# Attention: the PV matmuls of a half unit in two bursts instead of four single chunks

## The chip, the cores and the metric

One core of one Trainium2 chip runs the whole program. The metric is the device time of one execution in microseconds (us), the median of several runs; lower is better. Where a profile is shown, it is one profiled execution. The engines are TensorE (PE; its weight loads are shown apart as PEld), VectorE (DVE), ScalarE (ACT), GpSimd (POOL) and SyncE (SP), whose queue issues the DMAs.

## What is computed

Attention over 4 batches and 8 heads (sequence 576, head size 64) with a bias that depends on positions, then two MLPs one after the other on the attention's output (2304 tokens, width 512). All data are float32.

```python
scores = scale * np.matmul(q, k.transpose(0, 1, 3, 2))
...
scores = scores + bias.transpose(2, 0, 1)[None, :, :, :]
scores = scores - np.max(scores, axis=-1, keepdims=True)
attn = np.exp(scores)
attn = attn / (np.sum(attn, axis=-1, keepdims=True) + 1e-09)
return np.matmul(attn, v).astype(np.float32)
...
x = np.ascontiguousarray(attn_out.transpose(0, 2, 1, 3)).reshape(B * S, H * D)
x = _moe_ref(x=x, **moe_kwargs)
return _moe2_ref(x=x, **moe2_kwargs)
```

## The kernel before

The program has three stages: the bias tables (until about 85 us), the attention (until about 370 us) and the two MLPs. All three are written as one order of instructions by hand: each engine works through its own queue in the order in which the Python code issues, and semaphores between engines are set from the tiles that they share.

The attention works on 16 units. A unit is a pair of heads (0 to 3) and a batch (0 to 3), with 9 query tiles: tiles 0 to 7 are 128 queries of one of the two heads in turn, tile 8 is the last 64 queries of both heads together and has twice the score matmuls. The loop over `tau` takes one step for each tile of each unit (144 steps), and 16 steps more that drain the pipeline. `u, t = divmod(tau, 9)`. In step `tau` the code issues for tiles of different age:

- `expo` (L253, ACT), for the tile of two steps ago: the exponential, with its row sums; ahead of it nothing, behind it whatever copy out of PV was put off (`late`);
- `stats` and `norm` (L257, L258 on DVE; L263 on POOL), five steps old: the reciprocals, and the scaling of the tile;
- `settle5` (L308, ACT), eight steps old: copies the fifth transposes out of PSUM;
- `reduce_min` (L246, DVE), one step old: adds the bias to the scores, negates, takes the row minimum;
- `scores` (L231, PE), the tile of this step, into one of two PSUM buffers (`ps_s`); so a step's scores need the reduction of two steps ago;
- `settle` (L303; L301 for tile 8), eight steps old: copies four transposed blocks out of PSUM into `at`, on ACT for tiles 1, 3, 5, 7 and on DVE for the others;
- the PV steps, if any are in the list `pvq`;
- `transposes` (L273, four blocks; L277 a fifth one, called F in the prediction, after each odd tile; L281 and L282 for tile 8), seven steps old, into one of two PSUM buffers.

Then follow casts of the next units' queries and keys (`high` on ACT or DVE, `low` on POOL), their loads, and parts of the MLP weights' preparation (L490 ACT; L505, L506, L507, L503 DVE; L523 ACT; L521 POOL).

PV is done per half unit: half 0 are the queries of tiles 0 to 3 (N = 256), half 1 those of tiles 4 to 8 (N = 320). When the last tile of a half is settled (tile 3 or 8), `pv_steps` appends six entries to `pvq`: chunks 0 to 4 and `evac`. Chunk 0 (L320) is one matmul with a full 128x128 weight. Each of the chunks 1 to 4 (L323) is two matmuls, one for each head, with a 128x64 weight each (shown as 128\*64): the first head's output goes to the first 64 partitions of the accumulator, the second's to the other 64. In float32 one matmul is recorded as two, so a chunk has four records. The accumulator is one PSUM buffer (`ps_v`, one buffer). `evac` (L327, ACT) copies it out and stores it to `xs` in DRAM; it isn't issued where it is popped, but in the next step behind `expo`.

What the change touches is how many entries of `pvq` are taken in a step: one, or two where more than four are in the list, and none behind an `evac`. With six entries for each half, and a half finished every five or four steps, chunks 0 and 1 come in one step, chunks 2, 3 and 4 in one step each, `evac` in the next; eight of a unit's nine steps have a PV chunk.

In the steps from 140 on `tail` starts the MLPs between the last steps of the attention (`AT`): loads of their input `xm` from `xs` (L561), their split (L567 ACT, L568 POOL), and the first blocks of matmuls `up` (L582), which share PE, ACT, DVE and POOL with what the attention still has.

Of the kernel before, what the change touches and what calls it, by code (L numbers as in the profile page):

```python
# [126 lines left out]
def attention_phase(tc, qT, kT, vP, ident_d, par, c_log, bsc, xs, after_bias, load_weight, filler, tail):  # L127
# [4 lines left out]
    with ExitStack() as st, ExitStack() as early:  # L132
        right = lambda n, k: st.enter_context(tc.tile_pool(name=n, bufs=k, side="right"))
        vp, np_, sm, xp = right("p1v", 4), right("p1n", NBUF), right("p1m", 3), right("p1x", 2)
        left = lambda n, k: early.enter_context(tc.tile_pool(name=n, bufs=k))
# [98 lines left out]
        def reduce_min(u, t):  # L234
            s = sc.pop((u, t))
            if t == 8:
                n = np_.tile([128, S], F32, name="n8", bufs=1)
            else:
                if t % 2 == 0:
                    npair[u, t // 2] = np_.tile([128, 2 * S], F32, name="n")  # L240
                n = npair[u, t // 2][:, S * (t % 2):S * (t % 2) + S]
            if t % 3 == 0:
                nmin[u, t // 3] = sm.tile([128, 3], F32, name="mn")
                nsum[u, t // 3] = sm.tile([128, 3], F32, name="sums")
            m = nmin[u, t // 3][:, t % 3:t % 3 + 1]
            V.tensor_tensor_reduce(n.rearrange("p (a b) -> p a b", a=2), s[:, :, 0:288],  # L246
                                   bias[t].rearrange("p (a b) -> p a b", a=2), -0.125, 3.0e38, ALU.add, ALU.min, m)
            ntile[u, t] = n

        def expo(u, t):  # L250
            n = ntile[u, t]
            m = nmin[u, t // 3][:, t % 3:t % 3 + 1]
            A.activation(n, n, AF.Exp, bias=m, scale=-1.0, accum_out=nsum[u, t // 3][:, t % 3:t % 3 + 1])  # L253

        def stats(u, g):
            r = sm.tile([128, 3], F32, name="rec")
            V.tensor_scalar(r, nsum[u, g], 1e-9, None, ALU.add)  # L257
            V.reciprocal(r, r)  # L258
            nrec[u, g] = r

        def norm(u, t):
            n = ntile[u, t]
            G.tensor_scalar(n, n, nrec[u, t // 3][:, t % 3:t % 3 + 1], 1.0, ALU.mult, ALU.mult)  # L263
# [32 lines left out]
        def settle(u, t):  # L296
            o, i = place(at[u, min(t // 4, 1)][0], t, tr.pop((u, t)))
            copy = A.copy if t in ON_ACT else V.tensor_copy
            if t == 8:
                for c in range(0, 4, 2):  # L300
                    copy(o[:, c:c + 2], i[:, c:c + 2])  # L301
            else:
                copy(o, i)  # L303

        def settle5(u, t):
            if t in (1, 3, 5, 8):
                o = place5(at[u, min(t // 4, 1)][1], t)
                (A.copy if t in ON_ACT5 else V.tensor_copy)(o, tf.pop((u, t))[:, 0:o.shape[1]])  # L308

        def pv_steps(u, g):  # L310
            hp, b = units[u]
            v = vs.pop(u) if g else vs[u]
            main, rest = at[u, g]
            N = GW[g]
            p = []

            def mm(c):
                if c == 0:
                    p.append(ps_v.tile([128, 512], F32, name="pv"))
                    T.matmul(p[0][:, 0:N], v[:, 4].rearrange("p a d -> p (a d)"), rest, start=True, stop=False)  # L320
                    return
                for a in range(2):
                    T.matmul(p[0][64 * a:64 * a + 64, 0:N], v[:, c - 1, a], main[:, c - 1, a * N:a * N + N], start=False, stop=(c == 4))  # L323

            def evac():
                x = xp.tile([128, 320], F32, name="x")
                A.copy(x[:, 0:N], p[0][:, 0:N])  # L327
                c0 = b * S + 256 * g
                nc.sync.dma_start(xs[128 * hp:128 * hp + 128, c0:c0 + N], x[:, 0:N])
            return [lambda c=c: mm(c) for c in range(5)] + [evac]  # L330

        pvq, late = [], []
        for tau in range(NU * 9 + TAIL):
            u, t = divmod(tau, 9)
            for _ in range(PER[min(tau, len(PER) - 1)]):
                next(bias_steps, None)
            if tau == LAG - 1:
                assert next(bias_steps, 1) == 1
                p0.close()
                at_pool = right("p1a", 1)  # L340
                ps_t, ps_f, ps_v = psr(st, "ps_t", 2), psr(st, "ps_f", 1), psr(st, "ps_v", 1)

            def at_lag(lag):
                z = tau - lag
                return divmod(z, 9) if 0 <= z < NU * 9 else None
            y = at_lag(2)
            if y:
                expo(*y)
            for f in late:
                f()  # L350
            late = []
            y = at_lag(LAG - 2)
            if y:
                if y[1] % 3 == 0:
                    stats(y[0], y[1] // 3)
                norm(*y)
            z = at_lag(LAG + 1)
            if z:
                settle5(*z)
            y = at_lag(1)  # L360
            if y:
                reduce_min(*y)
                hp, b = units[y[0]]
                if b == NB - 1 and hp + 1 < NP:
                    load_bias(hp + 1, y[1])
            if tau < NU * 9:
                scores(u, t)
            if z:
                settle(*z)
            for _ in range(2 if len(pvq) > 4 else 1):  # L370
                if pvq:
                    f = pvq.pop(0)
                    if f.__name__ == "evac":
                        late.append(f)
                        break
                    f()
            if z and z[1] in (3, 8):
                pvq += pv_steps(z[0], z[1] // 8)
            y = at_lag(LAG)
            if y:  # L380
                transposes(*y)
            if t == 0 and u + 1 < NU:
                alloc(u + 1)
            if t == 6 and u + 1 < NU:
                load_v(u + 1)
            for n, i in ((u + 1, HIGH.get(t)), (u, HIGH.get(t + 9))):
                if i is not None and 1 <= n < NU:
                    high(n, i)
            for n, i in ((u + 1, LOW.get(t)), (u, LOW.get(t + 9))):
                if i is not None and 1 <= n < NU:  # L390
                    low(n, i)
                    if n + 1 < NU:
                        load_raw(n + 1, i)
            if tau < NU * 9:
                filler(t)
            if tau == NU * 9:
                early.close()
            tail(tau - NU * 9)


TAIL = 16
NBUF = 5
EBUF = 4
LR = (16, 19, 22, 25)
# [477 lines left out]
```

## Time and profile before

| | us |
|---|---|
| median of 3 runs | 1243.32 (1241.55 to 1244.18) |
| the profiled execution, its own time | 1237.99 |
| its span, first to last instruction | 1236.2 |

| engine | busy us | share of the span |
|---|---|---|
| PE (matmuls) | 1208.7 | 98% |
| PEld (weight loads) | 1044.5 | 84% |
| DVE | 726.0 | 59% |
| ACT | 646.0 | 52% |
| POOL | 566.2 | 46% |

The table counts an engine as busy from an instruction's start to its end; matmuls are pipelined, so that PE shows as busy also where two of them overlap only a little. The shares are over all three stages. For one stage one reads the table of stretches (busy time of each engine between two times), the waits in that stretch, and the timeline, where the distance from the start of one group of matmuls to the start of the next tells what the group costs PE, whatever the lengths of its records.

### The profile page before, as it was taken

What the parts mean: (1) busy time and instruction counts of PE and PEld (TensorE: products, weight loads), DVE (VectorE), ACT (ScalarE), POOL (GpSimd) and SP (SyncE); (2) the same over time, 40 slices, a digit from 0 to 9 for tenths busy, and PEclk for the clock granted to TensorE, in tenths of its full rate; (3) what the DMA queues carried; (4) which work ended last, traced back from release to release, by engine and by line L of the source; (5) the groups of instructions that cost most, each with busy time, mean ns of one, the idle gap of its engine ahead of it and who ended that gap; (6) DMA issues with size and microseconds to landing.
All of it is one profiled execution on the core that took longest, in us unless ns stands there. A gap on an engine that the chain in (4) does not pass through costs nothing.

```text
span 1236.2 us, 21193 instructions
## 1 busy us (share of the span) xinstructions
PE 1208.7 (98%) x7856; PEld 1044.5 (84%) x7856; DVE 726.0 (59%) x1292; ACT 646.0 (52%) x1338; POOL 566.2 (46%) x584
## 2 busy tenths in 40 slices
PE   7899999999989999999999999999999999999998
PEld 2257666666659999999999999889999999999997
DVE  7898878888738988988988668961101111111010
ACT  6897777778737667677666555332112211221111
POOL 1059888888635555565555335452122221222211
PEclk9999999999999999999999999999999999999999
DMA  5765746474211333333343223421001010010000
GB/s 192 245 199 159 217 138 202 140 214 148 88 53 60 113 120 106 104 120 120 128 145 116 98 69 108 153 73 35 27 10 35 2 35 26 10 35 10 26 18 17
DMA packets 80631, 120.86 MB, mean 98 GB/s; under 512 B 10256, under 2 KB 55056, under 8 KB 80528
## 3 DMA queue, kind: packets, MB, share of 16 engines
q1 hardware_dynamic: 80528, 119.51, 30.7%
q8 instruction: 62, 1.02, 0.3%
q14 instruction: 41, 0.34, 0.1%
HBM read 89.71 MB, written 29.77 MB: 97 GB/s over the span
## 4 chain that ended last, share of the span: by engine, by line
PE 66%; DVE 3%; DMA 1%; ACT 1%; issue 1%; POOL 0%; SPq 0%; DVEq 0%; ACTq 0%; POOLq 0%
PE up L582 38%; PE acc L659 16%; PE acc L667 11%; DMA wraw<-in_wo 1%; DVE wu L507 1%; DVE wu L503 1%; DVE wu L506 0%; PE pv L323 0%; DVE wu L505 0%; DMA wraw<-in_wv 0%; ACT wu L490 0%; ACT z L601 0%; DMA xm<-xs 0%; POOL xt L568 0%; DVE o L685 0%
## 5 line engine op out<-in xcount | busy, mean ns | idle before, releaser
L582 PE MATMUL up<-xt,w 128*128 128x256 f32 (+1 forms) x3744 | 536.2, 299 | 3.9 <-DVE t L627 1.9
L582 PEld LDWEIGHTS up<-xt,w 128*128 128x128 f32 x3744 | 524.7, 190 | 15.9 <-DVE t L629 4.5
L637 POOL TENSOR_TENSOR gl<-t,gh 128x256 fp32r<-128x256 f32 (+1 forms) x204 | 184.4, 914 | 468.9 <-ACT gh L636 301.4
L629 DVE TENSOR_TENSOR t<-up,t 128x256 f32<-128x256 f32 x108 | 45.5, 422 | 318.9 <-ACT t L608 318.9
L608 ACT ACTIVATE t<-up 128x256 f32<-128x256 f32 x108 | 41.5, 384 | 327.9 <-PE up L582 327.9
L659 PE MATMUL acc<-gh,w 128*128 128x384 f32 x768 | 195.7, 335 | 2.9 <-ACT z L601 2.9
L659 PEld LDWEIGHTS acc<-gh,w 128*128 128x128 f32 x768 | 138.0, 188 | 4.7 <-ACT z L601 3.8
L667 PE MATMUL acc<-w,gh 128*128 128x512 f32 x432 | 135.6, 395 | 0.0
L263 POOL TENSOR_SCALAR n<-n,rec 128x576 f32<-128x576 f32 x144 | 114.8, 809 | 43.3 <-DVE rec L258 30.0
L659 PE MATMUL acc<-gl,w 128*128 128x384 f32 x384 | 128.4, 334 | 0.0
L253 ACT ACTIVATE n<-n,mn 128x576 f32<-128x576 f32 x144 | 112.1, 779 | 26.1 <-DVE mn L246 26.0
L246 DVE CUSTOM_DVE_ANT_0 n<-sc,bias 128x576 f32<-128x576 f32 x144 | 107.5, 747 | 15.4 <-PE sc L231 11.5
L273 PEld LDWEIGHTS pt<-ident,n 128*128 128x128 f32 x576 | 60.6, 140 | 54.9 <-issue 39.7
L568 POOL TENSOR_TENSOR xt<-xm,xt 128x384 fp32r<-128x384 f32 (+1 forms) x84 | 75.5, 911 | 68.0 <-ACT xt L567 68.0
L521 POOL TENSOR_TENSOR w<-wu,w 128x512 fp32r<-128x512 f32 x68 | 98.2, 1445 | 12.4 <-ACT w L523 11.0
L636 ACT CAST gh<-t 128x256 fp32r<-128x256 f32 (+1 forms) x204 | 91.4, 454 | 7.6 <-PE acc L659 3.6
L273 PE MATMUL pt<-ident,n 128*128 128x128 f32 x576 | 94.1, 286 | 0.9 <-DVE at L303 0.9
L323 PE MATMUL pv<-at,vs 128*64 128x320 f32 (+1 forms) x512 | 90.9, 436 | 0.0
L622 ACT ACTIVATE z<-z,c 128x768 f32<-128x768 f32 x48 | 45.2, 941 | 77.4 <-DVE up L621 77.4
L623 DVE TENSOR_TENSOR t<-up,t 128x768 f32<-128x768 f32 x48 | 45.9, 956 | 65.3 <-ACT t L601 65.3
L667 PE MATMUL acc<-w,gl 128*128 128x512 f32 x216 | 84.0, 389 | 0.0
L667 PEld LDWEIGHTS acc<-w,gh 128*128 128x128 f32 x432 | 74.5, 190 | 9.8
(70 smaller groups left out, 1683.9 us busy)
## 6 DMA issues: line engine op xcount, KB each, us to landing
wraw<-in_wo SPq DMA_DIRECT2D x28, 512.0 KB, 3.8
bsc<-e SPq DMA_DIRECT2D x36, 295.5 KB, 2.8
raw<-in_qT SPq DMA_DIRECT2D x64, 144.0 KB, 3.5
raw<-in_kT SPq DMA_DIRECT2D x64, 144.0 KB, 3.1
xm<-xs SPq DMA_DIRECT2D x48, 192.0 KB, 3.7
x2s<-o SPq DMA_DIRECT2D x48, 192.0 KB, 3.8
wraw<-in_wi SPq DMA_DIRECT2D x16, 512.0 KB, 4.3
wraw<-in_wg SPq DMA_DIRECT2D x12, 512.0 KB, 3.7
```

The source lines that it names most:

```text
L246: V.tensor_tensor_reduce(n.rearrange("p (a b) -> p a b", a=2), s[:, :, 0:288], bias[t].rearrange("p (a b) -> p a b", a=2), -0.125, 3.0e38, ...
L253: A.activation(n, n, AF.Exp, bias=m, scale=-1.0, accum_out=nsum[u, t // 3][:, t % 3:t % 3 + 1])
L263: G.tensor_scalar(n, n, nrec[u, t // 3][:, t % 3:t % 3 + 1], 1.0, ALU.mult, ALU.mult)
L273: T.transpose(pt[:, i], n[:, o:o + 128], ident)
L323: T.matmul(p[0][64 * a:64 * a + 64, 0:N], v[:, c - 1, a], main[:, c - 1, a * N:a * N + N], start=False, stop=(c == 4))
L521: self.nc.gpsimd.tensor_sub(w[:, 1], u, w[:, 0].bitcast(F32))
L568: G.tensor_sub(t[:, 1], m, t[:, 0].bitcast(F32))
L582: T.matmul(p[:, 0:TB], w[:, a, 128 * kt:128 * kt + 128], x[:, c], start=(kt == 0 and i == 0), stop=(kt == 3 and i == 2))
L636: A.copy(h, x[:, j])
L637: G.tensor_sub(l, x[:, j], h.bitcast(F32))
L659: T.matmul(ac[blk][d][:, 0:TB], w[:, a, 128 * d:128 * d + 128], c, start=(begin and j == 0 and i == 0), stop=(end and j == NPR - 1 and i = ...
L667: T.matmul(ac[blk][d], g[:, c], w[:, a], start=(begin and i == 0), stop=(end and i == 2))
```

## The change

The number of entries taken from `pvq` now follows a counter of steps since the half was finished. One step after it three entries are taken (chunks 0, 1 and 2), two steps after it none, three steps after it three (chunks 3 and 4, and `evac`, which as before is put off to the next step). In all other steps none is taken. Lines of the MLP stage have numbers higher by 3 in the changed kernel (L567 is its L570).

```diff
--- before.py
+++ after.py
@@ -329,7 +329,7 @@
                 nc.sync.dma_start(xs[128 * hp:128 * hp + 128, c0:c0 + N], x[:, 0:N])
             return [lambda c=c: mm(c) for c in range(5)] + [evac]
 
-        pvq, late = [], []
+        pvq, late, pv_turn = [], [], 9
         for tau in range(NU * 9 + TAIL):
             u, t = divmod(tau, 9)
             for _ in range(PER[min(tau, len(PER) - 1)]):
@@ -367,7 +367,8 @@
                 scores(u, t)
             if z:
                 settle(*z)
-            for _ in range(2 if len(pvq) > 4 else 1):
+            pv_turn += 1
+            for _ in range(PV_BURST.get(pv_turn, 0)):
                 if pvq:
                     f = pvq.pop(0)
                     if f.__name__ == "evac":
@@ -376,6 +377,7 @@
                     f()
             if z and z[1] in (3, 8):
                 pvq += pv_steps(z[0], z[1] // 8)
+                pv_turn = 0
             y = at_lag(LAG)
             if y:
                 transposes(*y)
@@ -399,6 +401,7 @@
 
 
 TAIL = 16
+PV_BURST = {1: 3, 3: 3}
 NBUF = 5
 EBUF = 4
 LR = (16, 19, 22, 25)
```

In the order of PE's rows, the first half of the last unit but one, before. `sc` are scores, `kh` and `kl` the two parts of the keys, `pv` the PV accumulator, `at` the settled transposes, `pt` and `pf` the transposes in PSUM:

```order
L320 MATMUL pv_4416<-a50_4278,vs_4028 128x256
L323 MATMUL pv_4416<-at0_4277,vs_4028 64x256 x2
L273 MATMUL pt_4420<-ident_111,n_4264 128x128 x4
L231 MATMUL sc_4436<-kh_4115,qs_4114 128x288 x2
L231 MATMUL sc_4436<-kl_4116,qs_4114 128x288 x2
L323 MATMUL pv_4416<-at0_4277,vs_4028 64x256 x2
L273 MATMUL pt_4444<-ident_111,n_4264 128x128 x4
L277 MATMUL pf_4449<-ident_111,n_4264 128x128
L231 MATMUL sc_4458<-kh_4115,qs_4114 128x288 x2
L231 MATMUL sc_4458<-kl_4116,qs_4114 128x288 x2
L323 MATMUL pv_4416<-at0_4277,vs_4028 64x256 x2
L273 MATMUL pt_4466<-ident_111,n8_4319 128x128 x4
```

The last visit of this half stands one step further on, so chunks 1 to 4 are in four steps. After, the same half:

```order
L320 MATMUL pv_4397<-a50_4281,vs_4033 128x256
L323 MATMUL pv_4397<-at0_4280,vs_4033 64x256 x4
L273 MATMUL pt_4403<-ident_111,n_4222 128x128 x4
L277 MATMUL pf_4408<-ident_111,n_4222 128x128
L231 MATMUL sc_4416<-kh_4117,qs_4116 128x288 x2
L231 MATMUL sc_4416<-kl_4118,qs_4116 128x288 x2
L273 MATMUL pt_4422<-ident_111,n_4269 128x128 x4
L231 MATMUL sc_4438<-kh_4117,qs_4116 128x288 x2
L231 MATMUL sc_4438<-kl_4118,qs_4116 128x288 x2
L323 MATMUL pv_4397<-at0_4280,vs_4033 64x256 x4
L273 MATMUL pt_4448<-ident_111,n_4269 128x128 x4
```

Chunks 1 and 2 stand in one run of 64-column matmuls and chunks 3 and 4 in another, and the step between them has none. This holds for every half.

At the end of the attention, PE's rows of the last score tile and behind it, before:

```order
L231 MATMUL sc_4503<-kl_4116,qs_4114 128x64
L273 MATMUL pt_4515<-ident_111,n_4340 128x128 x4
L277 MATMUL pf_4520<-ident_111,n_4340 128x128
L320 MATMUL pv_4531<-a54_4375,vs_4028 128x320
L323 MATMUL pv_4531<-at4_4374,vs_4028 64x320 x2
L273 MATMUL pt_4535<-ident_111,n_4384 128x128 x4
L323 MATMUL pv_4531<-at4_4374,vs_4028 64x320 x2
L273 MATMUL pt_4552<-ident_111,n_4384 128x128 x4
```

And after:

```order
L231 MATMUL sc_4506<-kl_4118,qs_4116 128x64
L320 MATMUL pv_4518<-a54_4380,vs_4033 128x320
L323 MATMUL pv_4518<-at4_4379,vs_4033 64x320 x4
L273 MATMUL pt_4524<-ident_111,n_4342 128x128 x4
L277 MATMUL pf_4529<-ident_111,n_4342 128x128
L273 MATMUL pt_4537<-ident_111,n_4389 128x128 x4
L323 MATMUL pv_4518<-at4_4379,vs_4033 64x320 x4
```

The accumulation of the half before now starts between the last scores and the transposes behind them, where it stood behind these transposes, and has two chunks there.

ScalarE's rows at the casts of the MLP input (`xt<-xm`), before:

```order
L567 CAST xt_4593<-xm_4588 128x384
L308 COPY a50_4491<-pf_4557 128x128
L303 COPY at0_4490<-pt_4552 128x4x128
L327 COPY x_4651<-pv_4531 128x320
L308 COPY a54_4605<-pf_4620 128x128
L303 COPY at4_4604<-pt_4615 128x4x128
```

And after:

```order
L570 CAST xt_4597<-xm_4592 128x384
L327 COPY x_4600<-pv_4518 128x320
L308 COPY a50_4494<-pf_4561 128x128
L303 COPY at0_4493<-pt_4556 128x4x128
L308 COPY a54_4610<-pf_4629 128x128
L303 COPY at4_4609<-pt_4624 128x4x128
L327 COPY x_4680<-pv_4618 128x256
```

The copy of the last unit but one's second half out of PV (`x<-pv`, N = 320) now stands ahead of the copies of the transposes, and the copy of the following half (N = 256), which stood behind the first MLP block's activations and casts, now stands among the attention's last copies.

## Rows read from the trace of the kernel before

**Rows 1.** The page's table of engines: busy us, share of the span, instructions.

```profile
PE 1208.7 (98%) x7856; PEld 1044.5 (84%) x7856; DVE 726.0 (59%) x1292; ACT 646.0 (52%) x1338; POOL 566.2 (46%) x584
```

**Rows 2.** Table of stretches, two successive units: us, busy (count) PE, PEld, DVE, ACT, POOL, clock, DMA.

```profile
184.56:202.04 17.48, 17.48 (x125) 12.00 (x124) 14.26 (x35) 13.55 (x34) 14.13 (x16) 1.00 0.69 208
202.04:219.52 17.48, 17.48 (x125) 12.00 (x124) 14.27 (x36) 13.96 (x34) 14.78 (x16) 1.00 0.69 212
```

**Rows 3.** Waits of PE's weight loader, 110 to 330 us: who <- whom, us, times, longest.

```profile
PEld pt L273 <- issue: 30.2, 68, 0.5
PEld pv L323 <- issue: 21.8, 100, 0.4
```

**Rows 4.** Timeline of PE, steps with a visit: start, length, line, out<-in, shape, count.

```profile
205.14 0.50 PE L231 MATMUL sc<-kh,qs 128*128 128x288 f32 x2
205.83 0.76 PE L323 MATMUL pv<-at,vs 128*64 128x320 f32 x4
206.52 0.66 PE L273 MATMUL pt<-ident,n 128*128 128x128 f32 x4
207.04 0.52 PE L231 MATMUL sc<-kh,qs 128*128 128x288 f32 x2
...
212.88 0.50 PE L231 MATMUL sc<-kh,qs 128*128 128x288 f32 x2
214.68 0.52 PE L231 MATMUL sc<-kh,qs 128*128 128x288 f32 x2
```

**Rows 5.** Timeline of PE, first unit, steps without a visit.

```profile
95.03 0.53 PE L231 MATMUL sc<-kh,qs 128*128 128x288 f32 x2
96.02 0.51 PE L231 MATMUL sc<-kh,qs 128*128 128x288 f32 x2
...
104.69 0.51 PE L231 MATMUL sc<-kh,qs 128*128 128x288 f32 x2
105.77 0.51 PE L231 MATMUL sc<-kh,qs 128*128 128x288 f32 x2
```

**Rows 6.** Timeline of PE, two windows in the run of four chunks at the attention's end.

```profile
369.84 0.70 PE L323 MATMUL pv<-at,vs 128*64 128x320 f32 x4
...
370.11 0.70 PE L323 MATMUL pv<-at,vs 128*64 128x320 f32 x4
```

**Rows 7.** Groups of VectorE, 110 to 330 us: count, busy us, mean ns, idle before, releasers.

```profile
L246 DVE CUSTOM_DVE_ANT_0 n<-sc,bias 128x576 f32<-128x576 f32 x113 | 84.4, 747 | 12.5 <-PE sc L231 9.1 <-issue 1.3 <-PE pt L273 0.9
L503 DVE SCALAR_TENSOR_TENSOR wu<-wraw,wu 128x512 int32<-128x512 int32 x12 | 15.7, 1306 | 0.0
```

**Rows 8.** Timeline of PE and ScalarE at the attention's end.

```profile
342.72 0.70 PE L320 MATMUL pv<-a,vs 128*128 128x320 f32 x2
344.05 0.66 PE L273 MATMUL pt<-ident,n 128*128 128x128 f32 x4
...
344.33 0.92 ACT L567 CAST xt<-xm 128x384 fp32r<-128x384 f32 x2
...
349.60 0.51 ACT L567 CAST xt<-xm 128x384 fp32r<-128x384 f32 x1 [0.79 <-DMA xm<-xs]
...
350.54 4.40 PE L582 MATMUL up<-xt,w 128*128 128x384 f32 x24
...
354.78 0.59 PE L320 MATMUL pv<-a,vs 128*128 128x256 f32 x2
...
359.77 4.45 PE L582 MATMUL up<-xt,w 128*128 128x384 f32 x24
...
366.06 1.21 PE L320 MATMUL pv<-a,vs 128*128 128x320 f32 x2 [1.84 <-ACT x L327]
...
370.74 0.44 PE L582 MATMUL up<-xt,w 128*128 128x384 f32 x1
```

**Rows 9.** Table of stretches there, behind PE's wait; PEclk is the number after POOL's.

```profile
366.00:368.00 2.00, 1.94 (x6) 0.80 (x8) 0.09 (x1) 0.01 (x1) 2.00 (x3) 0.58 0.22 56
```

**Rows 10.** Chain of work that ended last, the weights' stretch: start, us, what.

```profile
809.01 3.42 DMA wraw<-in_wo
```

## The prediction

> **What bounds the kernel now.** I first read the page's engine table: TensorE (PE) is busy for 98% of the span [rows 1]. Busy can hide waiting, so the next view is the table of stretches, one unit of the attention (nine steps) at a time: in two successive units PE is busy for all 17.48 us, VectorE for 14.3, ScalarE for 13.6 to 14.0, GpSimd for 14.1 to 14.8 [rows 2]. The waits between 110 and 330 us then hold no row of PE's matmuls, only rows of its weight loader: 100 waits before a PV matmul and 68 before a transpose whose cause is "issue", nothing that another engine did [rows 3]. So in this stage the time is the sum of what PE does, and PE itself leaves holes where it goes into the 64-column PV matmuls and where it comes out. The changed lines are in this stage alone.
>
> **The change, part by part.** No matmul is added or removed. A unit has two PV halves of five chunks; chunk 0 is a full-width matmul, chunks 1 to 4 are pairs of 64-column matmuls, one for each head, side by side. I call a run of 64-column matmuls within one step a visit. Before, a half makes four visits of one chunk; after, two of two chunks (the order of PE's rows shows it). Two visits fewer in each half, four in a unit.
>
> *What a visit costs.* A step with F (the fifth transpose) and one visit at N=320 lasts 207.04 - 205.14 = 1.90 us, at N=256 214.68 - 212.88 = 1.80 us [rows 4]; the same step without a visit lasts 105.77 - 104.69 = 1.08 us [rows 5]. So a visit of one chunk costs 0.82 and 0.72 us. A chunk is two pairs. Where four chunks already run behind one another in this trace, at the very end of the attention, pairs at N=320 start 370.11 - 369.84 = 0.27 us apart [rows 6]: 0.54 us for a chunk's streaming, and 0.43 at N=256 (estimate, by columns). What is left, 0.28 and 0.29 us, is going in and out, and is paid per visit, not per chunk. I take 0.285.
>
> *The sum in the steady stage.* 4 x 0.285 = 1.14 us per unit, 17.48 to 16.34. Up to the last score tile 29 halves are complete in both orders: 58 visits x 0.285 = 16.5 us. The bounds of this price: nothing, if a second chunk behind the first pays all that a visit does; 0.285 as taken. I take the upper end, since the row with chunks behind one another is the very form that the change makes.
>
> *What hides the rest.* All other engines have work of 13.6 to 14.8 us per unit and would have 16.3: covered on average. Within a unit it is uneven: steps without a visit last about 1.0 us (0.99 without F, [rows 5]), steps with a visit 2.2 to 3.7 (estimate: 1.80 + 0.43 at N=256; 1.90 + 0.54 at N=320, in the longest with chunk 0, 0.6, and with a second score tile, which up to PV takes 205.83 - 205.14 = 0.69). Scores of step T need the reduction of T-2 only, so VectorE may fall behind by about one step; short steps stand singly between long ones but for one pair. I take no new wait.
>
> *The copy out.* PV's single PSUM buffer is emptied one step after the last chunk instead of two. ScalarE's next work there is a copy of transposes that PE issues after that chunk, so it would have waited for PE anyway: nothing.
>
> *The end of the attention.* Here PE does wait, and the change moves things both ways [rows 8]. In the last score step a visit of three chunks now stands ahead of its transposes. Before, chunk 0 and one chunk took 344.05 - 342.72 = 1.33 us; with a second one about 1.9. ScalarE's last exponential, its casts of the MLP input (344.33) and the reload that ends in the last cast (349.60) follow those transposes, so all move 1.9 us. In ScalarE's order the copy out of PV then stands ahead of the two copies that PE needs (0.3), and PE has chunk 0, two chunks, transposes and F at N=256 before the first MLP matmul, which stood at 350.54 (estimate: 1.33 x 0.8 for chunk 0 and one chunk, 0.43 for the second, 0.5 for transposes and F, 2.0). Together that matmul comes 4.2 us later than the steady stage alone would put it. In return, between the first and the second MLP block PE had 359.77 - 354.78 = 5.0 us of PV and transposes and keeps two chunks in one visit and three sets of transposes, 2.9 by the same durations (-2.1); its wait until 366.06 for the copy out of PV goes, as that copy is now far ahead (-2.0); and after that wait the granted clock was 0.58 [rows 9], so that chunk 0 and four chunks took 370.74 - 366.06 = 4.7 us, where 0.27 us per pair gives about 3.0 (-1.7). That is -1.6. But PE now stands idle for about 5 us ahead of the first MLP matmul; in this trace a wait of 1.84 us was enough for the clock to be at its lower level (1.2 GHz) behind it, so the +1.7 may come back there, or a little more. I take 0 for the end, bounds -1.6 and +2.
>
> *After it* the chain of waits is PE's MLP matmuls, later VectorE's weight conversion with DMA between [rows 10]. That conversion is handed out per MLP step, so it moves along with the steps.
>
> **The sum:** -16.5. The profiled execution took 1237.99 us, so 1221.5; the median of the three runs is 5.3 us higher, 1243.32, and I keep that distance: **1226.8**. Own range 1223.5 to 1230 (the end's bounds and 1.5 us between runs).
>
> **A rule that speaks against it.** The rows of the run of four chunks show pairs spaced at their streaming time. The Trainium skill (TensorE: Matmul & The Clock Gate, "The mechanism" in Part 3) says that a weight load overlaps with running matmuls only when the row group differs; here all loads use all 128 rows, so by that rule they would stand bare in a burst too. The trace disagrees at N=320; no run here shows it at N=256. It makes the first rival.
>
> **The rivals.**
> 1. *The loads stand bare in a burst.* Within a visit 206.52 - 205.83 = 0.69 us pass from its first matmul to the next transpose [rows 4], 0.15 more than the streaming. If that recurs with each chunk, a removed visit saves 0.13 us: 58 x 0.13 = 7.5, 1235.8. For it: N=256 was not seen in a run. Against it: [rows 6].
> 2. *ScalarE becomes the bound in part.* Its copies of odd tiles now wait for transposes at the end of long steps, with an exponential of 0.8 us, a cast and the copy out queued behind. If it comes late to the copies that the first chunks of a visit need by 0.4 us, once per half, 29 x 0.4 = 11.6 us go: 1238.4; half of that 1232.6. Against it: it has 2.3 us per unit to spare.
> 3. *The end costs more*: clock at the lower level through the first MLP block and none of the idle time recovered: +2 to +4, so 1229 to 1231.
> 4. *The gain is lost later*: if the weight conversion and its DMAs were tied to absolute time, PE would wait there for what it won: about 1243. Against it: loads start only when the conversion before is done.
> 5. *Slower: VectorE is starved in the long steps and overrun in the short ones.* In a short step it has, for example, a reduction (0.75) and a weight instruction (1.31) [rows 7], 2.05 us against 1.0: 1 us short, in four of the five short steps, 4 us per unit. It decides from where more than 1.14 us of these 4 isn't absorbed by the two score buffers. With half absorbed: (2.0 - 1.14) x 14.5 = +12.5 us, 1255.8. Against it: the reduction stands first in VectorE's step, and a long step follows nearly each short one.
>
> That the change doesn't do what it says is excluded by the order of the rows.
>
> **How the numbers follow.** Forecast 0.70, rival 1 0.07, rival 2 0.09, rival 3 0.06, rival 4 0.04, rival 5 0.04. A measurement of this kernel can tell about 0.2%, 2.5 us, from no change: faster than 1240.8 are the forecast, rivals 1 to 3: 0.92; within it rival 4: 0.04; slower rival 5: 0.04. The range, 1222 to 1236, holds the forecast, rivals 1 and 3 and the milder half of rival 2.
>
> **What would show it.** Right: a unit takes 16.3 us (three steps between 2.2 and 2.7, one near 3.7, five near 1.0 to 1.4); the weight loader's waits before PV fall from about 100 to a half in the same units; PE has no row in the waits there; pairs inside a burst start 0.27 and 0.21 us apart. Wrong: pairs of a second chunk with holes (rival 1); waits of PE for ScalarE's copies (rival 2) or VectorE's reductions (rival 5); the first MLP matmul later than 350.54 - 16.5 + 4.2 = 338.2 by more than 1 us, or a longer stretch at the lower clock there (rival 3); waits of PE for converted weights that the trace of before does not have (rival 4).

## The result and the profile after

The changed kernel takes 1225.97 us (median of 6 runs, 1222.77 to 1227.02); the kernel before 1242.43 (6 runs, 1236.90 to 1244.55: three run beside it and the three known before). The ratio is 0.9872, 95% interval 0.9846 to 0.9899: 16.5 us faster. The forecast was 1226.8, in a range of 1222 to 1236. The profiled execution took 1225.91 us (span 1224.1), where that of before took 1237.99.

The page's engine table of the changed kernel, columns as in [rows 1]: PE is busy for 16.3 us less, with the same number of instructions.

```profile
PE 1192.4 (97%) x7856; PEld 1053.9 (86%) x7856; DVE 731.8 (60%) x1292; ACT 641.1 (52%) x1338; POOL 570.5 (47%) x584
```

The table of stretches, two successive units, columns as in [rows 2]:

```profile
184.41:200.75 16.34, 16.34 (x125) 12.47 (x124) 15.03 (x36) 13.42 (x33) 14.81 (x16) 1.00 0.73 201
200.75:217.09 16.34, 16.34 (x125) 12.47 (x124) 15.05 (x36) 13.27 (x33) 14.81 (x16) 1.00 0.87 248
```

A unit lasts 16.34 us in place of 17.48, to the hundredth what was forecast, and PE is still busy in all of it. VectorE, with the same 36 instructions, shows 15.0 us of work where it showed 14.3 [rows 2]; this comes back below.

Waits of the weight loader, 110 to 330 us (who <- whom, us, times, longest), against [rows 3]:

```profile
PEld pv L323 <- issue: 8.6, 40, 0.3
PEld pt L273 <- POOL n L263: 7.2, 15, 0.5
...
PEld pv L323 <- DVE rec L258: 5.7, 13, 0.4
```

100 waits before a PV matmul have become 54 (40, 13 and one more of 0.4 us; which engine a wait as short as this is put down to says little). The 220 us hold 12.6 units of before and 13.5 of the changed kernel, so that is 7.9 waits per unit against 4.0: one for each visit. PE's matmuls have no row among the waits of this stage.

Timeline of PE: a visit of two chunks at N=320, with the transposes behind it, and one at N=256 (start, length, line, out<-in, shape, count):

```profile
202.43 1.30 PE L323 MATMUL pv<-at,vs 128*64 128x320 f32 x8
203.66 0.65 PE L273 MATMUL pt<-ident,n 128*128 128x128 f32 x4
...
206.26 1.08 PE L323 MATMUL pv<-at,vs 128*64 128x256 f32 x8
207.28 0.66 PE L273 MATMUL pt<-ident,n 128*128 128x128 f32 x4
```

Two chunks hold PE for 203.66 - 202.43 = 1.23 us, where one held it for 0.69 [rows 4]: the second adds 0.54, its streaming and nothing else. (Eight records are two chunks; the prediction calls the two heads' records that run side by side a pair, so a chunk is two pairs, 0.27 us each.) At N=256 two take 207.28 - 206.26 = 1.02.

The span falls into four stages. Each pair of columns sets two profiled executions side by side: the first pair, and one more of each kernel (below, before_again and after_again).

| us | before | after | difference | again, before | again, after | difference | forecast |
|---|---|---|---|---|---|---|---|
| to the first scores of the fourth unit | 115.40 | 119.05 | +3.65 | 116.21 | 116.31 | +0.10 | +0.3 |
| from there to the last unit's first scores | 209.76 | 196.08 | -13.68 | 209.78 | 196.08 | -13.70 | -13.7 |
| from there to the third MLP block | 45.58 | 42.73 | -2.85 | 43.83 | 42.59 | -1.24 | -3.1 |
| from there to the end of the span | 865.47 | 866.23 | +0.76 | 865.56 | 866.33 | +0.77 | 0 |
| sum | 1236.2 | 1224.1 | -12.1 | 1235.4 | 1221.3 | -14.1 | -16.5 |

The last column is the prediction's own sum, laid on these stages: 48 of the 58 visits lie in the second row; of the other ten five lie ahead of it and five behind. At a unit's start the new order has 1.7 us of PV behind it that the old one still has before it (0.6 for chunk 0, 0.54 for each of two chunks), so the first row is 1.7 - 5 x 0.285 = +0.3 and the third -1.7 - 1.4 = -3.1.

The end of the attention, timeline of PE:

```profile
328.38 0.43 PE L231 MATMUL sc<-kh,qs 128*128 128x288 f32 x3
...
339.45 1.22 PE L320 MATMUL pv<-a,vs 128*128 128x256 f32 x2 [4.94 <-ACT a L308]
340.60 1.98 PE L323 MATMUL pv<-at,vs 128*64 128x256 f32 x8
343.42 4.44 PE L585 MATMUL up<-xt,w 128*128 128x384 f32 x24
...
350.63 4.46 PE L585 MATMUL up<-xt,w 128*128 128x384 f32 x24
...
355.56 2.37 PE L323 MATMUL pv<-at,vs 128*64 128x320 f32 x16
357.86 4.43 PE L585 MATMUL up<-xt,w 128*128 128x384 f32 x24
```

And the table of stretches there (PEclk is the number after POOL's):

```profile
340.00:342.00 2.00, 2.00 (x10) 0.77 (x8) 0.00 (x0) 0.00 (x0) 2.00 (x3) 0.50 0.82 259
```

PE waits 4.94 us for one of ScalarE's copies, and behind that the granted clock is 0.50, the lower of the two levels: chunk 0 lasts 1.22 us in place of 0.59, two chunks 1.98 in place of 1.08. The third block then follows without the wait that stood there before [rows 8].

### The profile page after: what moved, and what is told of

It is laid out like the page before. It is cut to its first block, busy times and chain, and to the rows that moved or that the text cites. A ratio compares the mean times of both kernels' runs of the same rounds, so it can differ in the third digit from the quotient of the medians.

```text
span 1224.1 us, 21207 instructions
## 1 busy us (share of the span) xinstructions
PE 1192.4 (97%) x7856; PEld 1053.9 (86%) x7856; DVE 731.8 (60%) x1292; ACT 641.1 (52%) x1338; POOL 570.5 (47%) x584
## 3 DMA queue, kind: packets, MB, share of 16 engines
q8 instruction: 62, 1.02, 0.4%
## 4 chain that ended last, share of the span: by engine, by line
PE 88%; DVE 5%; DMA 3%; ACT 2%; issue 1%; SPq 0%; POOL 0%; DVEq 0%; ACTq 0%; POOLq 0%
PE up L585 39%; PE acc L662 15%; PE acc L670 11%; PE sc L231 7%; PE pv L323 6%; PE pt L273 6%; PE bt L71 2%; PE pv L320 1%; DMA wraw<-in_wo 1%; DMA bsc<-e 1%; DVE y L66 1%; DVE wu L510 1%; DVE wu L506 1%; DMA wraw<-in_wv 1%; PE pf L277 1%
## 5 line engine op out<-in xcount | busy, mean ns | idle before, releaser
L585 PEld LDWEIGHTS up<-xt,w 128*128 128x128 f32 x3744 | 524.7, 190 | 16.3 <-DVE t L632 5.4
L632 DVE TENSOR_TENSOR t<-up,t 128x256 f32<-128x256 f32 x108 | 45.6, 423 | 319.4 <-ACT t L611 319.4
L263 POOL TENSOR_SCALAR n<-n,rec 128x576 f32<-128x576 f32 x144 | 117.6, 828 | 26.2 <-ACT n L253 18.4
L246 DVE CUSTOM_DVE_ANT_0 n<-sc,bias 128x576 f32<-128x576 f32 x144 | 107.3, 745 | 22.4 <-POOL n L263 13.5
L273 PE MATMUL pt<-ident,n 128*128 128x128 f32 x576 | 90.9, 281 | 0.0
L273 PEld LDWEIGHTS pt<-ident,n 128*128 128x128 f32 x576 | 66.8, 142 | 27.6 <-POOL n L263 7.9
L231 PE MATMUL sc<-kh,qs 128*128 128x288 f32 x336 | 81.2, 327 | 3.5 <-DVE mn L246 3.2
```

Source lines behind the costliest of these rows:

```text
L231: T.matmul(s[:, hf, x:x + n], w, k_[:, a, y:y + n], start=(i == 0), stop=(i == len(ops) - 1 and x + n == S // 2))
L273: T.transpose(pt[:, i], n[:, o:o + 128], ident)
L585: T.matmul(p[:, 0:TB], w[:, a, 128 * kt:128 * kt + 128], x[:, c], start=(kt == 0 and i == 0), stop=(kt == 3 and i == 2))
```

## The experiments

All kernels were timed beside the kernel before. "Unit" is the distance between the first scores of successive units in the steady stage, from each kernel's own trace.

| kernel | visits per unit | unit, us | time, us (runs) | ratio to before, 95% |
|---|---|---|---|---|
| before | 8 | 17.48 | 1239.8 to 1242.4 (medians of five sets) | 1 |
| three_visits | 6 | 16.94 | 1233.82 (6) | 0.9944 [0.9924, 0.9965] |
| full_between | 6 | 16.98 | 1235.07 (8) | 0.9956 [0.9939, 0.9972] |
| changed kernel | 4 | 16.34 | 1225.97 (6) | 0.9872 [0.9846, 0.9899] |
| after_again | 4 | 16.34 | 1225.17 (5) | 0.9872 [0.9847, 0.9897] |
| uneven | 4 | 16.34 to 16.38 | 1225.17 (5) | 0.9879 [0.9858, 0.9901] |
| tail_old | 4 | 16.34 | 1227.08 (6) | 0.9892 [0.9867, 0.9917] |
| after_cast | 4 | 16.34 | 1222.37 (4) | 0.9850 [0.9827, 0.9872] |
| mixed | 3 | 16.21 to 16.42 | 1224.02 (5) | 0.9875 [0.9847, 0.9903] |
| mixed_cast | 3 | 16.05 to 16.12 | 1220.61 (5) | 0.9843 [0.9819, 0.9868] |
| one_burst | 2 | 16.23 to 16.41 | 1226.07 (5) | 0.9886 [0.9864, 0.9908] |
| one_burst_cast | 2 | 15.95 to 16.03 | 1219.48 (5) | 0.9831 [0.9811, 0.9852] |
| late_casts | 2 | 15.95 to 16.03 | 1212.61 (5) | 0.9792 [0.9769, 0.9816] |

### Is it the visits? Three per half, a visit cut in two, an uneven cut

three_visits:

```diff
-PV_BURST = {1: 3, 3: 3}
+PV_BURST = {1: 3, 2: 1, 3: 2}
```

> Three visits per half: chunks 0 to 2 in the first step after the half is finished, chunk 3 in the second, chunk 4 and the copy out in the third. Theory (price per visit): 29 x 0.285 = 8.3 us more than the changed kernel, 1234.3 us, a unit of 16.91 us, half way between the two kernels. Rival (the gain comes from the steps left free of PV, or from the earlier copy out): as the first chunk and the copy out stand where the changed kernel has them and only the free step between is filled, either the whole gain or none of it would go: 1226 or 1242 us.

1233.82 us, a unit of 16.94: half way, as by the price per visit.

full_between, which leaves every matmul in its step and moves chunk 0 between chunks 1 and 2 (the lines left out make chunk 1 start the accumulation):

```diff
...
-            return [lambda c=c: mm(c) for c in range(5)] + [evac]
+            return [lambda c=c: mm(c) for c in (1, 0, 2, 3, 4)] + [evac]
```

> The same matmuls in the same steps as in the changed kernel, but the full-width chunk 0 stands between chunks 1 and 2 and not ahead of them, so that the first run of 64-column matmuls is cut in two. Theory (the price is for going into and out of the 64-column form): one visit more per half, 8.3 us more than the changed kernel, 1234.3 us, a unit of 16.91 us. Rival (what is paid is a step's having PV in it at all: its place between scores and transposes, the copies waited for): no difference, 1226.0 us and a unit of 16.34 us.

1235.07 us, a unit of 16.98: 0.64 us more per unit for two runs of 64-column matmuls more, 0.32 each. Its timeline shows the first burst at N=256, cut in two:

```profile
209.22 0.51 PE L231 MATMUL sc<-kh,qs 128*128 128x288 f32 x2
...
209.92 0.65 PE L324 MATMUL pv<-at,vs 128*64 128x256 f32 x4
210.50 0.70 PE L321 MATMUL pv<-a,vs 128*128 128x256 f32 x2
211.13 0.65 PE L324 MATMUL pv<-at,vs 128*64 128x256 f32 x4
211.72 0.66 PE L273 MATMUL pt<-ident,n 128*128 128x128 f32 x4
...
212.24 0.51 PE L231 MATMUL sc<-kh,qs 128*128 128x288 f32 x2
```

From the first chunk to the transposes 211.72 - 209.92 = 1.80 us. In the changed kernel the two chunks in one piece took 1.02 (above) and chunk 0 206.26 - 205.74 = 0.52:

```profile
205.13 0.51 PE L231 MATMUL sc<-kh,qs 128*128 128x288 f32 x2
...
205.74 0.59 PE L320 MATMUL pv<-a,vs 128*128 128x256 f32 x2
...
207.80 0.52 PE L231 MATMUL sc<-kh,qs 128*128 128x288 f32 x2
```

So 0.26 us more for the same three chunks; another 0.09 stands ahead of them, as the scores are now followed by a 64-column matmul. The whole step, from scores to scores, takes 212.24 - 209.22 = 3.02 us in place of 207.80 - 205.13 = 2.67, so 0.35 more, and the same step at N=320 takes 221.82 - 217.84 = 3.98 in place of 217.09 - 213.39 = 3.70, so 0.28. No step was filled or emptied, and chunk 0 is of the same float32 data as the other chunks, so the price is paid for going into the 64-column form and out of it. The Trainium skill (TensorEngine Tiling (Array Packing), "Key Properties") says that changing the tiling mode drains TensorE. A price at each change of width agrees with that, here 0.28 to 0.35 us for both ways; that it is a drain no trace here shows.

uneven:

```diff
-PV_BURST = {1: 3, 3: 3}
+PV_BURST = {1: 2, 3: 4}
```

> Two visits per half as in the changed kernel, but cut unevenly: chunks 0 and 1 in the first step, chunks 2, 3 and 4 in the third. Theory (price per visit, not per chunk): the same as the changed kernel, 1226.0 us, a unit of 16.34 us. Rival (second and later chunks of a visit have a price of their own, or the longest step sets waits of other engines): a difference of over 2 us either way.

1225.17 us, a unit of 16.34 to 16.38: the same as the changed kernel. How the chunks are shared out between two visits makes no difference that can be seen; the number of visits does.

### How far does it go? One burst, and a cast taken from VectorE

one_burst:

```diff
-PV_BURST = {1: 3, 3: 3}
+PV_BURST = {1: 6}
```

> All five chunks of a half and the copy out are taken one step after the half is finished: one visit per half instead of two. Theory (a visit has a fixed price of 0.285 us on TensorE, whatever it holds): 29 halves x 0.285 = 8.3 us less than the changed kernel, about 1217.7 us, a unit of 15.77 us in the steady stage. Rival (with so little left, VectorE, busy for 46.1 of 50 us in the steady stage of the changed kernel, becomes the bound, and TensorE waits for its reductions in the four short steps that now follow one another): a unit of 16.0 to 16.6 us, 1221 to 1230 us, with rows of TensorE among the waits for VectorE.

The rival held: 1226.07 us, a unit of 16.32 in the mean. Two visits less per unit brought nothing. The tables of stretches, 135 to 315 us, of the changed kernel and of one_burst:

```profile
135.00:315.00 180.00, 180.00 (x1346) 137.46 (x1347) 165.48 (x388) 147.53 (x363) 163.16 (x166) 1.00 0.61 178
```

```profile
135.00:315.00 180.00, 177.38 (x1348) 140.32 (x1347) 171.91 (x386) 147.52 (x364) 163.24 (x167) 1.00 0.60 176
```

VectorE is now busy for 171.91 of 180 us, and PE no longer for all of it. Waits of PE and of its loader in these 180 us, and five rows of the timeline:

```profile
PEld sc L231 <- DVE mn L246: 5.2, 11, 0.5
PE sc L231 <- DVE mn L246: 2.6, 11, 0.3
```

```profile
202.88 0.15 DVE L257 TENSOR_SCALAR rec<-sums 128x3 f32<-128x3 f32 x1
...
203.22 0.76 DVE L246 CUSTOM_DVE_ANT_0 n<-sc,bias 128x576 f32<-128x576 f32 x1
...
204.04 0.53 PE L231 MATMUL sc<-kh,qs 128*128 128x288 f32 x2 [0.30 <-DVE mn L246]
...
212.81 1.24 DVE L257 TENSOR_SCALAR rec<-sums 128x3 f32<-128x3 f32 x1
...
213.87 0.20 ACT L253 ACTIVATION_READ_ACCUMULATOR n<-n,mn 128x1 f32 x1
```

Eleven units, eleven waits of PE for a reduction. And not all that VectorE shows as busy is work: L257, on 128x3 elements, lasts 1.24 us at 212.81 and 0.15 us at 202.88. It ends about when ScalarE has read the sums that it needs (213.87 + 0.20). So VectorE stands behind ScalarE for a microsecond with its next reductions queued behind. The same is why it showed 15.0 us in the changed kernel without more to do: from 110 to 330 us L257 lasts 0.155 us in the mean before and 0.45 in the changed kernel, 0.9 us more per unit.

mixed keeps one burst for the first half of a unit and two for the second:

```diff
...
-PV_BURST = {1: 3, 3: 3}
+PV_BURST = {1: 6}, {1: 3, 3: 3}
...
-            for _ in range(PV_BURST.get(pv_turn, 0)):
+            for _ in range(PV_BURST[pv_half].get(pv_turn, 0)):
...
-                pv_turn = 0
+                pv_turn, pv_half = 0, z[1] // 8
```

> The first half of a unit (N=256) gives its five chunks in one burst, the second half (N=320) keeps its two bursts: three visits per unit where the changed kernel has four. In the kernel with one burst for both halves TensorE's wait for VectorE's reduction stood only where the second half's second burst was taken away (steps 0 to 2 of a unit then are all short); in the first half four short steps followed one another without a wait. Theory: this kernel pays for one visit less and has no such wait, a unit of 16.34 - 0.285 = 16.05 us, 14.5 x 0.285 = 4.1 us less than the changed kernel, about 1221.8 us. Rival (any long run of short steps makes VectorE late, as it is busy for 15.0 of 16.3 us): a unit of 16.3 us, 1226 us, with TensorE waiting for reductions in steps 4 to 7.

The rival again: 16.21 to 16.42. The wait was not bound to the place that I had named. The time, 1224.02, can't be told from the changed kernel's.

Then VectorE was relieved by its one cast of the keys per unit, in the kernels with two, three and four visits (one_burst_cast, mixed_cast, after_cast):

```diff
-            if i == 3:
-                V.tensor_copy(o, raws[u, i])
-            else:
-                A.copy(o, raws[u, i])
+            A.copy(o, raws[u, i])
```

> One burst per half as before, and the one cast of the keys that VectorE does in each unit (0.99 us, fourth part of the next unit's queries and keys) goes to ScalarE, which does the other three in 0.67 us each. ScalarE then has 13.4 + 0.7 = 14.1 us per unit, VectorE some 14.6 in place of 15.6. Theory (with fewer than four visits per unit VectorE sets the pace): the unit falls from 16.32 us towards TensorE's own 15.77, to 15.8 to 16.0, so 4.5 to 8 us less than with one burst alone, 1218 to 1222 us. Rival (the unit of 16.3 us is held by something else, the two score buffers or ScalarE's order): a unit of 16.3 us or more, 1226 us or more.

> Three visits per unit (first half one burst, second half two), and VectorE's cast of the keys on ScalarE. Theory (VectorE set the pace at 16.31 us, a visit fewer counts 0.285 once it is relieved): a unit of 16.05 us, 14.5 x 0.285 = 4.1 us less than the changed kernel, 1221 to 1222 us. Rival (something else holds the unit): 16.3 us, 1224 to 1226 us.

> The changed kernel with VectorE's cast of the keys on ScalarE and nothing else. Theory (with four visits per unit TensorE alone sets the pace): a unit of 16.34 us as in the changed kernel, the time the same within 1.5 us, 1224 to 1227 us. Rival (VectorE was already holding the changed kernel back): a unit below 16.3 us, 1222 us or less.

With three visits the unit falls to 16.05, the price of the visit to the hundredth; with two to 15.95, 0.18 above TensorE's own 15.77 (an estimate by the price of a visit); with four it stays at 16.34. The stretch of one_burst_cast:

```profile
135.00:315.00 180.00, 179.99 (x1377) 143.00 (x1375) 161.61 (x386) 155.42 (x382) 164.60 (x168) 1.00 0.60 175
```

PE is full again and VectorE has 161.61. (Its wait for ScalarE's sums is still there, 6.4 us in these 180, but now shows as idle time, and L257 lasts 0.16 us in the mean.) So VectorE's queue was what held the unit at 16.3, and in the changed kernel PE and VectorE were about level. after_cast was to be the same in time. Its unit is, but its median is 2.8 to 3.6 us below those of the two sets of the changed kernel, below what its theory allowed and just short of its rival; the 95% intervals of the ratios overlap, and in the profiled executions its span, 1221.0 us, is that of after_again, 1221.3. So no gain in time is shown. The start is taken up below.

### The start: the same kernels again

> The changed kernel once more, to see what its start does. In its first profile the second unit lasted 19.46 us, where the kernel before had 16.83, with VectorE waiting 2.4 us for a load of the bias (4.6 us from issue to landing, before 3.3). Theory (the load's time differs from run to run, the change has no part in it): another length of the second unit here, by up to 3 us, and a wait for the bias that differs by as much. Rival (the bursts cause it): 19.4 to 19.5 us and a wait of 2.4 us again.

> The kernel before once more, for the same question. Theory (run to run): a second unit longer than 16.83 us, with a wait for the bias, can be seen here too. Rival (the bursts cause it): 16.8 us again, no wait for the bias.

The second unit lasts 17.73 us in after_again (first profile 19.46) and 17.48 in before_again (first 16.83). VectorE's reduction that waited for the bias, in the changed kernel and in after_again:

```profile
86.16 0.76 DVE L246 CUSTOM_DVE_ANT_0 n<-sc,bias 128x576 f32<-128x576 f32 x1 [2.37 <-DMA bias<-bsc]
```

```profile
83.53 0.76 DVE L246 CUSTOM_DVE_ANT_0 n<-sc,bias 128x576 f32<-128x576 f32 x1 [0.75 <-DMA bias<-bsc]
```

The same program waits 2.37 us in one execution and 0.75 in another, so the 3.65 us of the first table are for the most part that execution's. Even units that are alike to the last instruction differ: the first, which has no PV, lasts 20.07 us in the changed kernel's profile and 21.46 in that of tail_old. What stays open: neither profile of before has this wait, while of the eight profiles of kernels with bursts and VectorE's cast left where it was seven have it (0.2 to 2.7 us; mixed has none), though these programs differ only behind it (the first PV matmul of the changed kernel stands at 91.33 us). The four with the cast on ScalarE have none, which may be where after_cast's lower median is from; no run shows it.

### The end: the old order there, and a queue put right

tail_old keeps the bursts up to step 140:

```diff
-            for _ in range(PV_BURST.get(pv_turn, 0)):
+            for _ in range(PV_BURST.get(pv_turn, 0) if tau < 141 else 2 if len(pvq) > 4 else 1):
```

> The changed kernel's bursts up to step 140; from step 141 on, which is from the second half of the last unit but one to the end of the attention, the entries are taken as in the kernel before. Theory (at the end the later start of the first MLP block is given back by the third): the first MLP matmul stands about 9 us behind the last score tile again, as before, not 15; the third block's first matmul stands where it stood, within 1 us; the time is that of the changed kernel within 1 us, 1225 to 1227 us. Rival (the 6 us that the first MLP matmul came later are lost): 3 to 6 us less, 1220 to 1223 us.

Neither came. The first MLP matmul did move up, to 10.7 us behind the last score tile from 15.0, but the time is no better, 1227.08 us:

```profile
338.08 6.97 PE L585 MATMUL up<-xt,w 128*128 128x384 f32 x24
...
349.88 4.45 PE L585 MATMUL up<-xt,w 128*128 128x384 f32 x24
356.18 0.81 PE L320 MATMUL pv<-a,vs 128*128 128x320 f32 x2 [1.84 <-ACT x L327]
356.92 4.07 PE L323 MATMUL pv<-at,vs 128*64 128x320 f32 x16
360.91 4.43 PE L585 MATMUL up<-xt,w 128*128 128x384 f32 x24
```

The first block, now straight behind the wait, lasts 6.97 us in place of 4.44, and the wait ahead of the third is back with a lower clock behind it. From the last unit's first scores the third block comes after 360.91 - 314.18 = 46.7 us, where the bursts gave 42.7. (It is not quite the old end: the old order's last accumulation stood one place later.) So an earlier first block is worth nothing by itself. In the profiled executions the bursts are the better end of the two by 4 us; the medians, 1.1 and 1.9 us apart, don't tell them apart.

What PE waits for there is a copy of ScalarE, and what ScalarE does before it is two casts that wait for a reload. late_casts is one_burst_cast with these two casts behind the copies:

```diff
         x_split(block(0), kt)
         if kt < 2:
             x_load(block(0), kt + 2)
+        if kt == 1:
+            yield
     yield
...
-AT = (-4, 1, 3, 7)
+AT = (-4, 1, 2, 3, 7)
```

> The kernel with one burst per half and the cast of the keys on ScalarE, and one thing more, at the end of the attention: the third and fourth cast of the first MLP input, which wait for a reload, stand behind ScalarE's two copies that TensorE needs for its last accumulation, not ahead of them. Theory (TensorE's wait of 5 us there, and the lower clock behind it, come from ScalarE standing in line behind that reload): no wait of 5 us before the last unit's first accumulation, the granted clock stays at 1.00 there, the first MLP matmul stands 9 to 12 us behind the last score tile in place of 17, and the total is 3 to 6 us below that of the kernel without this, 1213.5 to 1216.5 us. Rival (the wait moves to the first MLP matmul, which needs the fourth cast anyway, and the lower clock with it): the third MLP block starts within 1 us of where it stood, 1218.5 to 1220.5 us.

1212.61 us, 0.9792 of before: 6.9 us below one_burst_cast by the medians, 4.8 by the two ratios, and the fastest of all. The first MLP matmul stands 10.1 us behind the last score tile, where it stood 17.0. ScalarE and PE of one_burst_cast at the end of the attention (line numbers there are lower by 3):

```profile
330.53 0.51 ACT L567 CAST xt<-xm 128x384 fp32r<-128x384 f32 x1 [3.14 <-DMA xm<-xs]
...
331.66 0.51 ACT L567 CAST xt<-xm 128x384 fp32r<-128x384 f32 x1 [0.62 <-DMA xm<-xs]
332.08 0.26 ACT L305 COPY a<-pf 128x128 f32<-128x128 f32 x1
...
332.39 1.22 PE L317 MATMUL pv<-a,vs 128*128 128x256 f32 x2 [5.30 <-ACT a L305]
```

And late_casts:

```profile
326.12 0.27 ACT L305 COPY a<-pf 128x128 f32<-128x128 f32 x1
...
326.44 0.70 PE L317 MATMUL pv<-a,vs 128*128 128x256 f32 x2 [0.52 <-ACT a L305]
...
329.30 0.51 ACT L567 CAST xt<-xm 128x384 fp32r<-128x384 f32 x1 [2.42 <-DMA xm<-xs]
329.48 2.28 PE L582 MATMUL up<-xt,w 128*128 128x384 f32 x11
```

The tables of stretches, first one_burst_cast and then late_casts, behind the start of that accumulation:

```profile
332.00:334.00 2.00, 1.61 (x4) 0.80 (x6) 0.00 (x0) 0.82 (x3) 1.86 (x4) 0.50 0.34 96
```

```profile
326.00:328.00 2.00, 1.56 (x12) 0.94 (x14) 0.65 (x1) 0.88 (x3) 2.00 (x3) 1.00 0.07 9
```

ScalarE still waits for the reload, but the copy (L305) no longer waits with it. PE does its last accumulation during the reload, the granted clock stays at 1.00, and the third block starts 24.5 us behind the last score tile in place of 30.8, 6.2 us earlier. The gain was expected at 3 to 6 us.

## Why the prediction held, step by step

**The price of a visit** was right, 0.285 us. The steady stage gives (17.48 - 16.34) / 4 = 0.285, three_visits 0.30, full_between 0.32, mixed_cast against the changed kernel 0.29. The nine steps of a unit are as forecast too: three with a visit of 2.23 to 2.67 us, one of 3.70, five without of 0.95 to 1.39.

**A second chunk at its streaming time**: right at both widths, 0.54 us at N=320 and 0.43 at N=256 (1.02, less the 211.72 - 211.13 = 0.59 of one chunk in full_between). That settles the first rival: had the weight loads stood bare in a burst, the second chunk would have cost 0.69 at N=320. With it falls the rule of the Trainium skill that I had weighed (TensorE: Matmul & The Clock Gate, "The mechanism" in Part 3), as I had read it: these loads use all 128 rows and yet don't show.

**The other engines keep up**: right, but closer than I said. I took their busy time of 13.6 to 14.8 us per unit as the measure; one_burst shows that VectorE's floor by its queue, waits for ScalarE's sums included, is about 16.3. So there was next to no reserve behind the 16.34. The mechanism of the fifth rival exists; it decides from about a unit of 16.3 us on, just beyond this change.

**The copy out at no cost**: nothing speaks against it. PE has no wait in the stage, and the unit comes out to the hundredth.

**The end**: within the stated bounds in its sum, off in one term. The last score matmuls before stand at

```profile
341.49 0.44 PE L231 MATMUL sc<-kh,qs 128*128 128x288 f32 x3
```

and from there the first MLP matmul came 6.0 us later (343.42 - 328.38 = 15.04 us in place of 350.54 - 341.49 = 9.05), not 4.2. Of the 4.2 the last piece, chunk 0, two chunks, transposes and F at N=256, was put at 2.0 and took 343.42 - 339.45 = 3.97: I had let the lower clock fall on the first MLP block, and it fell on the accumulation ahead of it. From the last unit's first scores on, the third block comes 0.3 us later than forecast in the first pair of executions and 1.9 in the second. By the prediction's own sign (a first MLP matmul over 1 us behind 338.2; it stands at 343.42 and 340.56, 1.8 and 1.7 us of it by the end's own term, the rest from the start) the third rival is there in part, and beside the second pair the end costs nearly the 2 us that it began at. The difference between the pairs is the kernel before's: its wait of 1.84 us was followed by a clock of 0.58 [rows 9] in the one execution and of 1.00 in the other, where the accumulation took 369.82 - 366.78 = 3.0 us and not 4.7. I had counted that drop as part of the old kernel; it is part of some of its executions.

before_again, the wait and the table of stretches behind it:

```profile
366.78 0.81 PE L320 MATMUL pv<-a,vs 128*128 128x320 f32 x2 [1.84 <-ACT x L327]
```

```profile
366.00:368.00 2.00, 1.22 (x6) 0.64 (x8) 0.80 (x1) 0.72 (x3) 1.87 (x2) 1.00 0.00 0
368.00:370.00 2.00, 2.00 (x16) 0.90 (x12) 0.00 (x0) 0.07 (x1) 1.32 (x2) 1.00 0.72 173
```

**After it** nothing was to change; both pairs lose 0.8 us there. PE's waits for VectorE in the first MLP's activation (L632, before L629) are 2.8 us in the changed kernel's profile against 1.9 and 2.2 in the two of before, which would be most of it; it wasn't tried.

**From the profile to the median** the step failed, and this hid the rest. I kept the 5.3 us by which the median of the first three runs of before lay above its profiled execution. Over all runs on record (48 of before, 11 of the changed kernel) the medians are 1240.62 and 1225.83 us: the base of 1243.32 was 2.7 us too high, and the gain is 14.8 us (15.5 between the means), not 16.5. The two errors cancel to 1.0 us; that the forecast came so near is in this part luck. The profiled executions say the same of the gain: 12.1 us in the first pair and 14.1 in the second, 4.4 and 2.4 less than the sum.

Why before's runs spread, the record shows in part: it has the mean granted clock of each run, and the time goes with it. Of the 42 runs of before beside the experiments the eight at 1.000 took 1235.98 to 1240.02 us, the seven at 0.995 and 0.996 1243.47 to 1245.27. Both profiled executions are at the upper end of the clock (0.999 and 1.000). The eleven runs of the changed kernel all lie at 0.994 to 0.997, and both its profiles show the lower level at the attention's end. So before seems to escape in some of its runs a loss that the changed kernel has in each; where the clock falls in the runs that were not profiled isn't known.

## What to carry to other kernels

In this kernel matmuls in the 64-column form pay for going in and out, not for each of them, so where they must stand among full-width work, count the switches and put as many together as the other engines' queues can follow. Such a gain ends where the next engine's queue is full, and its busy time tells that point badly: look for its instructions that last many times longer than others of the same size, and move one operation before removing more switches. At the seam of two stages look at which instruction of another engine's queue stands waiting for a transfer ahead of the one that TensorE needs; here putting two casts behind two copies brought 5 to 7 us, and starting the next stage earlier nothing.

## What the runs showed of the hardware that I had not expected

- A wait of TensorE of the same length, 1.84 us at the same place of the same program, was followed by the lower clock level in one execution (0.58) and not in the other (1.00); tail_old, with the same wait, had 0.50 behind it. Waits of 4.5 to 5.3 us ahead of an accumulation were followed by 0.50 in all ten traces that have one.
- VectorE's busy time holds waiting: L257 on 128x3 elements shows 0.15 us or 1.24 us, as the sums are there or not. In one_burst_cast the same wait shows as idle time.
- A load of 288 KB of the bias from memory took 3.3 to 5.6 us from issue to landing in executions of programs that are alike up to there, and the second unit lasts from 16.8 to 20.4 us. Of the 2.8 us between the two spans of the changed kernel, 2.7 are there already at the fourth unit.
